# Paired stores at the end of a fused attention and gated feed-forward kernel, with a new order of all its work

## Chip, cores and metric

The kernel runs on one core of one Trainium2 chip. The metric is device time of one execution in microseconds. The engines are TensorE (PE in the profile, with its weight loads as PEld), VectorE (DVE), ScalarE (ACT), GpSimd (POOL) and SyncE (SP). Each runs its own instruction stream in program order and waits on semaphores that other engines raise. SP and POOL also issue the DMA transfers.

## What is computed

Two layers are fused. The first is attention over sequences projected to 64 keys (8 batches, 8 heads, 1024 tokens, 64 wide), the second a gated feed-forward layer on its 8192 tokens (512 to 1536 to 512).

```python
k_proj = einsum('ks,bhsd->bhkd', E, k)
v_proj = einsum('ks,bhsd->bhkd', F, v)
scores = (q @ k_proj^T) / 8
attn   = softmax(scores)                # over the 64 projected keys
x      = attn @ v_proj                  # as [8192, 512] tokens
out    = (sigmoid(x @ w_gate) * (x @ w_val)) @ w_out
```

Inputs and output are float32; the matrices are bfloat16 on the chip.

## The kernel before

The work goes batch by batch. A batch of 1024 tokens is two blocks of 512 tokens, so there are 16 blocks, numbered 0 to 15. For a batch, k and v are loaded and projected (`kv`, `apart`), K and Q are transposed, and four score tiles of 128 token groups go through `score_pair` (PE), `highest` (DVE, the maximum, L1609), `lower` (the subtraction, L1636 on DVE), `exps` (ACT), a DMA transpose on SP (`turn_p`), `outs` (PE), `invert` and `divide` (L1701, L1718; DVE or POOL), and a DMA transpose back (`turn_x`).

The feed-forward products use a seven-product scheme (Strassen's, in Winograd's form): a product of 2x2 sub-blocks takes seven block products instead of eight, with sums of operands before and of results after. For x @ w_gate and x @ w_val, `seven` issues per third of a block and per weight seven products named A11, A12, S2, S1, S3, A22, S4 (jobs GA11, VS4 and so on), each of four matmuls of 256 columns. Between them stand copies of PSUM banks on ACT (`snap`, `copy`, L532), additions on DVE (`plus`, L1104), the tanh on ACT and the gate product on DVE (`hidden`, L1173), which writes hT. For the output layer `o_jobs` issues seven products of twelve matmuls, each split into two jobs of six, with `snap`, `leave` and `copyO` on ACT, `merge` on DVE (L1376), and sums of hidden operands (`s_sum`, L547) on DVE, of which the fourth runs on POOL in three pieces in the inner blocks. The first block runs as plain products (`mm_one`, 512 columns, half products of two matmuls where weights arrive late). All matmuls are issued at L518, all ACT operations at L532.

Eight PSUM banks (pF0 to pF3, pA0 to pA3) and 13 SBUF buffers of 512 columns (EF's two halves and `spare`) hold the intermediate results. They are the scarce resource: a product may start when its bank was read out by the last copy, addition or gate that needs it.

The order is written out by hand of a search. Calls of `job` only collect jobs, each with its engine and body, in the order in which the source makes them. `Scheduler.run` then reads two constant lists. ORDER is a sequence of job numbers; the jobs of each engine are issued in the sequence in which they stand there, and a negative entry -m is a filler, which calls `busy`: one matmul of 256 m columns from the identity into bank 7, whose result nobody reads. PLACES gives every bank or buffer slot its number. `Plan.add` derives from the sequence which operation waits for which, by keys of what each reads and writes; `emit` turns this into semaphore waits (L129; SP's last waits, for the output, at L138).

The output leaves through `ost` (128 x 4 x 512, float32), four token tiles wide. Token tiles are named tt = 0 to 3; tok = tt // 2 is the token half of the scheme, and col = 0 or 1 the half of 512 columns. For blocks 0 to 14, `store` (L1259) sends one token tile of 512 columns, 256 KB, per issue on SP. For the last block `store_half` (L1271) sends one token tile of 256 columns, 128 KB, per issue, eight in all, in the order in which the quarters of the result are ready: (tok 1, col 1) and (tok 0, col 0), then (tok 1, col 0), then (tok 0, col 1), two token tiles each. The last quarter is merged in two pieces, so its two stores wait for one piece each. The kernel ends when SP has waited for the four semaphores out0 to out3.

Of the kernel before, what the change touches and what calls it, by code (L numbers as in the profile page):

```python
# [153 lines left out]
class Job:  # L154
# [191 lines left out]
class Scheduler:  # L346
# [4 lines left out]
    def job(self, eng, pos, body, release=0.0, name=""):  # L351
        self.jobs.append(Job(eng, body, name))
# [24 lines left out]
def bass_linformer_attn__then__ffn_glu_sigmoid_kernel(  # L377
# [20 lines left out]
    with contextlib.ExitStack() as es:  # L398
# [867 lines left out]
        def store_half(blk, tt, col):  # L1266
# [7 lines left out]
                cost=0.4,  # L1274
                nbytes=128 << 10,
            )

        def o_plain(blk, pos, step):
            h = hT[blk % 2]
            last = blk == 2 * B - 1  # L1280
# [616 lines left out]
```

## Time and profile before

| | |
|---|---|
| runs | 516.63, 516.04 and 516.71 us; median 516.63 |
| the profiled execution | 516.16 us, of which its span 514.4 us |
| instructions in the trace | 12647 |
| DMA packets | 140987, 71.60 MB |
| HBM | 60.29 MB read, 16.78 MB written |
| granted TensorE clock | 1.00 |

The span runs from the first to the last instruction of the program. Busy time of an engine is the time in which at least one of its instructions runs. For TensorE matmuls overlap: a matmul of 256 columns has a row of about 0.27 us, though the next one starts much sooner, so the rate is read from the starts of successive rows and not from their lengths. A timeline row gives start, length, engine, line, operation, output tile <- input tiles, shape and count; in brackets stands the idle time before it and what ended that. A row of a stretch gives, after its bounds and length, the busy time of PE, PEld, DVE, ACT and POOL, each with its number of instructions, then the granted clock, the share of DMA engines and GB/s. Names such as pA, pF, spare, ost are tiles without their numbers.

### The profile page before, as it was taken

To read this page: it belongs to the slowest core of one execution; us is meant where nothing else is said; L and a number is where in the kernel's file an instruction comes from. 1 tells how busy PE (TensorE), PEld (TensorE's weight loads), DVE (VectorE), ACT (ScalarE), POOL (GpSimd) and SP (SyncE) were. 2 spreads that over 40 slices of the span, in tenths; PEclk is the share of its full clock that TensorE was granted. 3 is DMA by queue.
4 is the path that set the end of the run, shared out by engine and by line. 5 is a ranking of instruction groups with operands and counts; after the bars stand their busy time and mean duration, and the time that the engine had idled before them with its cause. 6 is when DMAs were issued, how large, how long until landed. Compare 5 with 4: busy or idle time off the path is not lost.

```text
span 514.4 us, 12647 instructions
## 1 busy us (share of the span) xinstructions
PE 508.6 (99%) x4973; PEld 419.1 (81%) x4976; DVE 441.1 (86%) x858; ACT 372.7 (72%) x714; POOL 174.2 (34%) x200
## 2 busy tenths in 40 slices
PE   8999999999999999999999999999999999999997
PEld 4556858888888888888888888888888888888886
DVE  6779998699978997798996998979988899957885
ACT  1567776878887787866877777776888669668662
POOL 9894003623335016230244305350234301350020
PEclk9999999999999999999999999999999999999999
DMA  9999978899887448985699945998577932432004
GB/s 169 197 198 207 182 116 185 128 181 175 148 170 137 74 133 127 215 136 129 106 168 191 160 129 112 169 161 132 137 136 167 191 103 45 103 102 83 2 3 164
DMA packets 140987, 71.60 MB, mean 139 GB/s; under 512 B 97280, under 2 KB 133120, under 8 KB 140928
## 3 DMA queue, kind: packets, MB, share of 16 engines
q0 software_dynamic: 35936, 29.89, 38.9%
q1 hardware_dynamic: 104992, 40.91, 37.5%
q8 instruction: 39, 0.64, 0.5%
q14 instruction: 20, 0.16, 0.1%
HBM read 60.29 MB, written 16.78 MB: 150 GB/s over the span
## 4 chain that ended last, share of the span: by engine, by line
PE 98%; DVE 0%; ACT 0%; issue 0%; DVEq 0%
PE pA L518 51%; PE pF L518 48%; DVE hT L1173 0%; ACT EFT L532 0%; ACT spare L532 0%; ACT qT L532 0%; DVE ost L1376 0%; DVE warm L646 0%; DVE spare L1104 0%; DVE tV L647 0%; DVEq L129 0%
## 5 line engine op out<-in xcount | busy, mean ns | idle before, releaser
L532 ACT ACTIVATE spare<-pA 128x512 f32<-128x512 f32 (+2 forms) x169 | 95.7, 581 | 34.5 <-PE pA L518 22.5
L532 ACT ACTIVATE spare<-pF 128x512 f32<-128x512 f32 (+2 forms) x150 | 83.6, 570 | 33.9 <-PE pF L518 23.8
L547 POOL TENSOR_TENSOR hT<-hT,hS 128x512 bf16<-128x512 bf16 x42 | 48.7, 1174 | 123.2 <-PE pA L518 54.3
L1718 POOL TENSOR_TENSOR KVs<-spare,inv 128x384 bf16<-128x384 f32 (+1 forms) x51 | 37.9, 751 | 77.5 <-ACT spare L532 16.2
L1104 DVE TENSOR_TENSOR spare<-pA,spare 128x512 f32<-128x512 f32 x61 | 41.1, 682 | 15.2 <-PE pA L518 9.7
L532 ACT ACTIVATE spare<-spare 128x512 f32<-128x512 f32 x75 | 45.8, 627 | 2.4 <-DVE spare L1104 2.3
L1173 DVE SCALAR_TENSOR_TENSOR hT<-spare,pA 128x512 bf16<-128x512 f32 x57 | 38.6, 680 | 10.0 <-PE pA L518 8.7
L518 PE MATMUL pF<-wO,hT 128*128 128x256 bf16 (+1 forms) x310 | 43.8, 284 | 0.1
L518 PE MATMUL pA<-xT,wG 128*128 128x256 bf16 (+1 forms) x256 | 41.7, 286 | 0.0
L1173 DVE SCALAR_TENSOR_TENSOR hT<-spare,pF 128x512 bf16<-128x512 f32 x56 | 37.6, 679 | 3.5 <-PE pF L518 2.0
L518 PE MATMUL pA<-wO,hT 128*128 128x256 bf16 (+1 forms) x275 | 37.1, 277 | 0.1
L1104 DVE TENSOR_TENSOR spare<-pF,spare 128x512 f32<-128x512 f32 x50 | 33.9, 682 | 2.7 <-PE pA L518 1.3
L518 PEld LDWEIGHTS pF<-wO,hT 128*128 128x128 bf16 x312 | 30.1, 98 | 7.2 <-ACT pF L532 0.2
L518 PE MATMUL pF<-xT,wV 128*128 128x256 bf16 (+1 forms) x208 | 33.9, 285 | 0.0
L518 PE MATMUL pA<-xT,wV 128*128 128x256 bf16 (+1 forms) x200 | 32.4, 285 | 0.0
L518 PE MATMUL pA<-xS,wV 128*128 128x256 bf16 x208 | 31.0, 273 | 0.1
L518 PE MATMUL pA<-xS,tG 128*128 128x256 bf16 x208 | 31.1, 272 | 0.0
L559 POOL DMA_DIRECT2D Qb<-in_q_dram x18 | 14.2, 787 | 49.5 <-ACT ost L532 22.9
L518 PEld LDWEIGHTS pA<-wO,hT 128*128 128x128 bf16 x276 | 26.5, 98 | 4.3 <-issue 0.2
L518 PEld LDWEIGHTS pA<-xT,wG 128*128 128x128 bf16 x256 | 24.6, 98 | 6.1 <-ACT pA L532 0.3
L518 PE MATMUL pA<-xS,wG 128*128 128x256 bf16 x192 | 28.7, 273 | 0.0
L518 PE MATMUL pF<-wT,hT 128*128 128x256 bf16 x216 | 28.7, 273 | 0.0
(186 smaller groups left out, 1310.9 us busy)
## 6 DMA issues: line engine op xcount, KB each, us to landing
out_dram<-ost SPq DMA_DIRECT2D x60, 256.0 KB, 2.5
KVs<-in_v_dram POOLq DMA_DIRECT2D x15, 512.0 KB, 7.4
KVs<-in_k_dram POOLq DMA_DIRECT2D x14, 512.0 KB, 7.9
Qb<-in_q_dram POOLq DMA_DIRECT2D x14, 512.0 KB, 7.7
wO<-in_moe_w_out_dram POOLq DMA_DIRECT2D x1, 1536.0 KB, 18.7
KVs<-in_k_dram POOLq DMA_DIRECT2D x4, 256.0 KB, 6.4
Qb<-in_q_dram POOLq DMA_DIRECT2D x4, 256.0 KB, 8.5
wG<-in_moe_w_gate_dram POOLq DMA_DIRECT2D x4, 256.0 KB, 10.1
```

Of the source, the lines that this page charges most:

```text
L518: lambda e: e.matmul(o, lhsT, rhs, **kw),
L532: lambda e: e.activation(o, i, func, scale=scale),
L547: fn = lambda e: e.tensor_tensor(o, a, b, op)
L559: add("POOL", lambda e: e.dma_start(o, i), r=r, w=w, dma=sem, cost=0.78, nbytes=nbytes)
L1104: lambda e: e.tensor_tensor(PB(b)[:, :] if stay else BF(s), PB(b)[:, :], BF(s), ALU.add),
L1173: lambda e: e.scalar_tensor_tensor(o, y.rearrange("p (j c) -> p j c", j=2), 1.0, x.rearrange("p (j c) -> p j c", j=2), ALU.add, ALU.mult,),
L1718: fn = lambda e: e.tensor_tensor(xto.rearrange("p (g h d) -> p h g d", g=2, h=H)[:, hh[0] : hh[1], :, :], o[:, :, 0:DH].rearrange("p (h g) ...
```

## The change

For the last block the two token tiles of a quarter are sent by one issue (`store_pair`, 256 KB, 256 runs of 1 KB) for the first three quarters; the last quarter keeps its two single stores. So eight stores become five, and the job count goes from 2917 to 2914. The two constant lists are new: ORDER has 2942 entries instead of 2943, PLACES has 907 as before. No other line of the program changes.

In ORDER, most jobs stand near their old place: on TensorE 733 of 1039 jobs have another position among the jobs of their engine, by 1.9 places on average and 12 at most. The fillers are 22 entries -2 and six -1, where they were 20 and six.

```diff
 ORDER = (
-    16, -2, -2, -2, 17, 18, 4, 19, -2, -2, -2, -1, 28, 20, 29, 1, 30, 21, 31, -2, -1, 22, 0, 32, 2, 38, 33, -2,
...
+    2244, 2074, 2064, 2169, 2075, 2213, 2088, 2068, 2257, 2071, 2246, 2229, 2081, 2207, 2082, 2089, 2083, 2258,
...
 PLACES = (
-    0, 2, 4, 1, 1, 3, 5, 0, 6, 1, 0, 0, 2, 0, 1, 3, 3, 2, 4, 5, 4, 4, 0, 2, 5, 2, 4, 5, 5, 9, 7, 10, 3, 5, 4, 0,
...
+    0, 2, 6, 2, 1, 3, 5, 1, 4, 0, 2, 0, 0, 1, 3, 3, 6, 2, 1, 2, 1, 1, 2, 4, 2, 4, 0, 5, 5, 7, 4, 8, 7, 0, 0, 1,
...
+        def store_pair(blk, tok, col):
+            t = 4 * (blk % 2) + tok
+            cc = slice(256 * col, 256 * col + 256)
+            add(
+                "SP",
+                lambda e: e.dma_start(
+                    out_v[blk // 2, t : t + 3 : 2].rearrange("t p c -> p t c")[:, :, cc],
+                    ost[:, 2 * tok : 2 * tok + 2, cc],
+                ),
+                r=[("ost", 2 * tok + j, col) for j in range(2)],
+                dma=f"out{2 * tok}",
+                cost=0.4,
+                nbytes=256 << 10,
+            )
...
-            for i, tok, col in ((4, 1, 1), (4, 0, 0), (5, 1, 0), (6, 0, 1)) if last else ():
-                for tt in (2 * tok, 2 * tok + 1):
-                    job("SP", pos + step * i, lambda tt=tt, col=col: store_half(blk, tt, col), name="store")
+            for i, tok, col in ((4, 1, 1), (4, 0, 0), (5, 1, 0)) if last else ():
+                job("SP", pos + step * i, lambda tok=tok, col=col: store_pair(blk, tok, col), name="store")
+            for tt in range(2 * last):
+                job("SP", pos + step * 6, lambda tt=tt: store_half(blk, tt, 1), name="store")
```

Entries that the prediction speaks of, as they stand in the two lists for TensorE (numbers are jobs; 84 and 82 transpose Q of the first batch, 86 is a score tile, 143, 149 and 148 are half products of the first block, 2810 is the last product VS4, 2888 reads the gate that follows it):

```
old: 84, 82, 143, 86              new: 84, 82, 149, 148, 86
old: 2810, 2892, 2893, 2895, 2896, 2897, 2898, 2888     (2873 stands between 2810 and 2892)
new: 2810, 2895, 2897, 2898, 2888
```

357 rows, old and new, of tables (ORDER, PLACES) are left out of this document.

## The prediction

> **What bounds the kernel now.** I read the page first, then TensorE's waits, its timeline, and the queues at the end.
>
> ```profile
> span 514.4 us, 12647 instructions
> PE 508.6 (99%) x4973; PEld 419.1 (81%) x4976; DVE 441.1 (86%) x858; ACT 372.7 (72%) x714; POOL 174.2 (34%) x200
> PE 98%; DVE 0%; ACT 0%; issue 0%; DVEq 0%
> ```
>
> The chain that ended last is TensorE from end to end. The matmuls set the time, and an order can only change three things: filler matmuls, moments in which TensorE waits, and what follows its last matmul. The waits of TensorE by what ended them:
>
> ```profile
> PE pA L518 <- DVE tV L647: 1.1, 1, 1.1
> PE pF L518 <- DVE hT L1173: 0.4, 1, 0.4
> PE pA L518 <- ACT qT L532: 0.4, 1, 0.4
> PE pF L518 <- ACT EFT L532: 0.3, 1, 0.3
> ```
>
> That is 2.2 us, and the first 1.1 us is the start before any operand exists. Shorter waits hide in the pipeline: a matmul's row is longer than its issue slot, so I compare starts. The slot first, from the end, where six runs follow without a wait (one is quoted, with its successor):
>
> ```profile
> 508.48 1.47 PE L518 MATMUL pA<-wT,hT 128*128 128x256 bf16 x12
> 509.79 1.47 PE L518 MATMUL pF<-wO,hT 128*128 128x256 bf16 x12
> ```
>
> Twelve matmuls of 256 columns take 1.31 us from start to start, 0.109 us each; four take 0.44 us. Now places where four take longer:
>
> ```profile
> 97.06 0.60 PE L518 MATMUL pA<-xS,tV 128*128 128x256 bf16 x4
> 98.08 0.61 PE L518 MATMUL pF<-xS,wG 128*128 128x256 bf16 x4 [0.42 <-DVE hT L1173]
> ...
> 204.98 0.60 PE L518 MATMUL pA<-xS,wV 128*128 128x256 bf16 x4
> 205.49 0.60 PE L518 MATMUL pA<-xS,tG 128*128 128x256 bf16 x4
> ...
> 272.82 0.60 PE L518 MATMUL pA<-xS,tV 128*128 128x256 bf16 x4
> 273.46 0.61 PE L518 MATMUL pA<-xS,wG 128*128 128x256 bf16 x4
> ...
> 302.63 0.60 PE L518 MATMUL pA<-xT,wV 128*128 128x256 bf16 x4
> 303.12 0.83 PE L518 MATMUL pF<-wO,hT 128*128 128x256 bf16 x6
> ...
> 448.70 0.60 PE L518 MATMUL pA<-xT,wG 128*128 128x256 bf16 x4
> 449.27 0.60 PE L518 MATMUL pA<-xS,tG 128*128 128x256 bf16 x4
> ```
>
> Less 0.44, the waits are 0.58, 0.07, 0.20, 0.05 and 0.13 us. Going through the timeline after 50 us in this way, from the first of these places to the last, I find some twenty, about 2.5 us together. That sum is an estimate from starts that I do not all quote. So from 50 to 511 us an order can gain 2.5 us at most, and lose any amount.
>
> **The change part by part.** I read the two ORDER lists as instruction streams per engine: a non-negative number is a job, the jobs are those of the listing, and PLACES gives each job its bank and buffer. No job but the last stores is added or removed, and shape changes on TensorE (score pairs, projections) come in as many runs as before from the second batch on.
>
> *Filler.* The old list has 20 entries -2 and six -1, the new one 22 and six.
>
> ```profile
> L518 PE MATMUL pA<-ident 128*128 128x512 bf16 x20 | 6.0, 381 | 0.0
> ...
> 26.34 1.03 PE L518 MATMUL pA<-xT,wG 128*128 128x512 bf16 x4
> 27.20 1.03 PE L518 MATMUL pF<-xT,wV 128*128 128x512 bf16 x4
> ```
>
> A slot of 512 columns is (27.20 - 26.34) / 4 = 0.215 us, so two more cost 0.43 us. Below that it can only cost less, down to nothing where operands come late anyway. TensorE shows no wait on a load between 8 and 28 us, so I take **+0.43**.
>
> *First scores.* Scores 86 need the copies of transposes 82 and 84.
>
> ```profile
> 29.37 0.59 PE L518 MATMUL pF<-xT,wV 128*128 128x512 bf16 x2
> 30.36 0.38 PE L518 MATMUL pA<-kpD,qT 128*128 128x128 bf16 x4 [0.39 <-ACT qT L532]
> ```
>
> Between transpose and scores there lies one half product (143), two slots of 0.215 us, and TensorE starts 0.99 us after them instead of 0.43: 0.56 us lost, of which the row calls 0.39 waiting. In the new list two half products (149, 148) lie there. Two more slots cover 0.43: **-0.4** (between 0, if ACT comes later by as much, and -0.56).
>
> *Eight-matmul gaps.* Many waits in the fence are of one kind: a product ends, ACT copies its bank (snap, copyO, leaveO), and a matmul that needs the copy or the bank comes eight matmuls later.
>
> ```profile
> L532 ACT ACTIVATE spare<-pA 128x512 f32<-128x512 f32 (+2 forms) x169 | 95.7, 581 | 34.5 <-PE pA L518 22.5
> ```
>
> Eight slots are 0.87 us; the copy is 0.58, and the last matmul's row ends 0.16 after its slot (four have 0.60 for slots of 0.44). With two handoffs nothing is left, so each such place loses the 0.05 to 0.13 seen at 204.98, 302.63 and 448.70. After 45 us I count 20 places with only eight slots in the old lists (also counting what stands ahead of the copy on ACT), ten in the new, and one with less (scores 2401, about seven slots). Nine fewer at about 0.08: **-0.7**, between -1.2 and 0.
>
> *Waits that come of a queue.* Those at 97.06 and 272.82 are of DVE: the add or the gate was behind other work.
>
> ```profile
> 102.90:205.80 102.90, 102.90 (x1066) 88.20 (x1064) 93.92 (x181) 80.70 (x158) 33.25 (x38) 1.00 0.79 143
> L1104 DVE TENSOR_TENSOR spare<-pA,spare 128x512 f32<-128x512 f32 x61 | 41.1, 682 | 15.2 <-PE pA L518 9.7
> L1173 DVE SCALAR_TENSOR_TENSOR hT<-spare,pA 128x512 bf16<-128x512 f32 x57 | 38.6, 680 | 10.0 <-PE pA L518 8.7 <-PE pF L518 0.6 <-ACT spare L532 0.2
> L1609 DVE TENSOR_REDUCE topf<-pA 128x8 f32<-128x512 f32 x34 | 22.8, 681 | 0.7 <-PE pA L518 0.5
> ```
>
> DVE is busy 93.92 of 102.90 us there (third busy column), and each add (L1104), gate (L1173) or score maximum (L1609) takes 0.68 us, so one that waits for a later product holds up all behind it. Some 1.6 us of the 2.5 are of this kind. For the old waits I compared the slots between the product that the queue waits for and the matmul that needs it: at product 1629 they go from 16 to 20, at 1443 from 16 to 21, at 2485 from 8 to 24; at 1556 (272.82) they stay 22, and at 457 (97.06) they fall from 20 to 16 behind another gate. I take half of 1.6 as gone, -0.8, and +0.5 for waits in places that are now nearer: **-0.3**, with bounds of -1.6 and +3. The upper one is four late DVE operations of 0.68 that nothing covers.
>
> *Loads and transposes.* POOL issues all weight loads ahead of the sums of weights, and wO before batch 1's K.
>
> ```profile
> L559 POOL DMA_DIRECT2D wV<-in_moe_w_val_dram x8 | 6.4, 809 | 0.0
> ...
> DMA  9999999999999999999999999999999999999997
> ```
>
> The last line is the DMA share from 20 to 60 us: the engines are full, so what lands last does not move, and the weights that the new list uses earlier by more than a product (wV's third chunk, wG's fifth) also stand earlier in the queue. Zero, hidden by the plain products; a load that came late would cost at most one place in the queue, 0.8 us of issue. On SP one transpose of batch 2's Q now stands ahead of a store and of the last transpose of batch 1's probabilities. TensorE's list of waits has none on a DMA. Zero; uncovered, it is one issue.
>
> *The end.*
>
> ```profile
> 510.72 0.42 DVE L1376 SCALAR_TENSOR_TENSOR ost<-pF,EF 128x256 f32<-128x256 f32 x1 [1.01 <-PE pF L518]
> 511.37 0.42 DVE L1376 SCALAR_TENSOR_TENSOR ost<-pF,EF 128x256 f32<-128x256 f32 x1 [0.23 <-PE pF L518]
> ...
> 510.70 0.33 SPq L1271 DMA_DIRECT2D out_dram<-ost  x1
> 511.07 0.43 SPq L1271 DMA_DIRECT2D out_dram<-ost  x1
> 511.55 0.46 SPq L1271 DMA_DIRECT2D out_dram<-ost  x1
> 512.05 0.45 SPq L1271 DMA_DIRECT2D out_dram<-ost  x1
> ...
> out_dram<-ost SPq DMA_DIRECT2D x60, 256.0 KB, 2.5
> out_dram<-ost SPq DMA_DIRECT2D x8, 128.0 KB, 1.8
> ```
>
> The last merge ends at 511.79, but its store is issued at 512.05: SP was busy with the three ahead. With a pair in place of the two at 510.70 and 511.07, SP is free by about 511.15, the next half goes at its merge's end (511.14) and is through at 511.6, and the last goes at about 511.84: -0.2. An issue that finds SP idle took 0.33 instead of 0.45, which may give 0.1 more. Against it, the pair's 256 KB land in 2.5 us, from 510.70 at 513.2, beside the last halves; these moved as many bytes before, so I allow +0.2 for it. **-0.25**, between -0.4 and +0.2. The Trainium skill (DMA: Bandwidth & Descriptors, Anatomy of one DMA) has about 2 us of fixed time in every DMA, most of it the receipt of the write. By it merging removes nothing behind the last issue, and its formula gives 2.3 us for 128 KB, an estimate; the row of 128 KB stores has 1.8, so the trace agrees on the kind and is shorter. By this rule alone the term would be the -0.2 of the issue slots.
>
> The order just before the end changes too: the last product VS4 (job 2810) had 42 slots between it and output product 2888, which reads its gate; now it has 18, or 1.96 us. Add 0.68, gate 0.68, drain 0.16 and handoffs make 1.7. It fits by 0.3; one operation of DVE too many costs up to 0.4. Zero.
>
> Sum: +0.43 - 0.4 - 0.7 - 0.3 - 0.25 = **-1.2 us**, on a profiled execution of 516.16 us (span 514.4 and 1.8 around it). The runs shown have a median of 516.63; on that, 515.4.
>
> **The rivals.** *As many waits as before.* New near places take back what the eight-slot gaps and the queue give (-1.0 becomes 0): -0.2, 516.4. For it: such waits depend on all queues together, and I counted places, not queues. Against it: the eight-slot places really are half as many.
>
> *DVE's order makes new waits.* A gate or an add stands on DVE behind an operation whose product comes later; TensorE then loses one operation, 0.68 us, as at 98.08. The place is 103 to 309 us, where score maxima share DVE with the adds and gates. Two such waits undo the gain of 1.2; from four on the kernel is over 0.2% slower. Five give -1.2 + 3.4: 518.8; the likeliest of this case, four, 518.1. For it: DVE is at 91% there. Against: at the places I compared, the distances mostly grew.
>
> *POOL's sums meet DVE's.* The sum that frees the last output product runs on POOL in inner blocks.
>
> ```profile
> L547 POOL TENSOR_TENSOR hT<-hT,hS x42: 1142/1154/1597, 93.5 to 494.2; 128x512 bf16<-128x512 bf16 x42
> ```
>
> Most take 1.15 us, the slowest 1.60. If the new order puts a DVE sum beside each block's POOL sums, a chain of three can be 1.3 us late, as 3 times 0.44; two blocks whose matmuls do not cover it give 516.63 - 1.2 + 2.6 = 518.0, and below one block the forecast stands. The Trainium skill (SBUF — State Buffer, Who interferes with whom) says that a DVE operation with two SBUF inputs and a GpSimd operation that reads SBUF block each other for a whole instruction; the slowest row agrees.
>
> **How the numbers follow.** Forecast 0.40, faster, its own range 514.0 to 515.6. As many waits 0.28, within 0.2%. DVE's order 0.26, slower. POOL's sums 0.06, slower. A measurement of this kernel tells about 0.2%, 1.0 us, from no change. Of the forecast's case 0.02 ends within 0.2%, and 0.02 of the second faster. So faster 0.40, same 0.28, slower 0.32. The range begins where every term lies half way to its lower bound (0.2 - 0.5 - 0.95 - 0.95 - 0.3 = -2.5, so 514.1), rounded to 514.0; all lower bounds together (512.9) would need five lucky terms, and 0.06 is left out there. It ends at 518.4, between four and five uncovered DVE operations, and leaves out 0.12 above.
>
> **What would show it.** Fills: 22 rows of 128x512 from the identity. First scores: no wait on ACT qT over 0.1 at 30 us. Gaps: fewer starts late by 0.05 to 0.13. Queues: TensorE's list of waits without DVE hT of 0.4; several such rows would make the prediction wrong. End: last issue about 0.05 after the last merge, and span less last matmul at 2.9 us instead of 3.1.

## The result, and the profile after

| | before | after |
|---|---|---|
| median of all runs | 516.8 us (22 runs) | 514.86 us (22 runs) |
| middle half of the runs | 516.10 to 517.11 | 514.63 to 515.04 |
| the profiled execution | 516.16 us | 514.63 us |
| its span | 514.4 us | 512.8 us |

The ratio is 0.9965, with a 95% interval of 0.9955 to 0.9975: 1.8 us less (1.3 to 2.3). Forecast was 1.2 us less. The medians of the table differ by 1.9 us. Between the two profiled executions it is 1.53 us. The other 0.4 us of the medians' 1.9 is in the table's second row: the middle half of the runs of before is 1.0 us wide, and their median lies 0.6 above the execution that was profiled; that of after is 0.4 wide, and their median lies 0.2 above.

From the page of the changed kernel, the span, the busy times and the first line of the chain that ended last; then TensorE's waits (who waited, for whom: us in total, times, longest). After line 517 stands for 518 of before, 531 for 532; the lines behind the new function moved by 14 or 15.

```profile
span 512.8 us, 12657 instructions
PE 508.0 (99%) x4978; PEld 421.8 (82%) x4978; DVE 441.5 (86%) x858; ACT 371.2 (72%) x714; POOL 172.0 (34%) x200
PE 98%; DVE 2%; ACT 0%; issue 0%; DVEq 0%
```
```profile
PE pA L517 <- DVE tV L646: 1.1, 1, 1.1
PE pA L517 <- ACT spare L531: 0.6, 1, 0.6
PE pF L517 <- ACT EFT L531: 0.3, 1, 0.3
```

TensorE still ends last, but 2% of the chain is now VectorE: one wait there has grown large enough to lead the chain off TensorE. The waits for hT (0.4) and qT (0.4) of before are gone, and one of 0.6 for a copy in `spare` is new. The first scores, in the timeline:

```profile
29.57 0.59 PE L517 MATMUL pA<-xT,wV 128*128 128x512 bf16 x2
30.00 0.59 PE L517 MATMUL pF<-xT,wG 128*128 128x512 bf16 x2
30.43 0.39 PE L517 MATMUL pA<-kpD,qT 128*128 128x128 bf16 x4
```

Two half-products take 0.43 us each from start to start, and the scores follow with nothing lost, where before lost 0.56. The new wait, in the timelines of TensorE, VectorE, ScalarE and GpSimd:

```profile
370.49 0.60 PE L517 MATMUL pF<-xT,tV 128*128 128x256 bf16 x4
371.71 0.35 PE L517 MATMUL pA<-vpD,eT 128*128 128x130 bf16 x3 [0.62 <-ACT spare L531]
...
367.40 1.22 DVE L546 TENSOR_TENSOR hT<-hT 128x512 bf16<-128x512 bf16 x1
368.55 0.68 DVE L1624 TENSOR_REDUCE topf<-pF 128x8 f32<-128x512 f32 x1
...
371.06 0.17 DVE L1716 RECIPROCAL inv<-pA 128x4 f32<-128x4 f32 x1
...
371.27 0.88 ACT L531 ACTIVATE spare<-pA 128x260 f32<-128x260 f32 x2 [0.68 <-DVE inv L1716]
...
367.19 1.15 POOL L546 TENSOR_TENSOR hT<-hT,hS 128x512 bf16<-128x512 bf16 x1 [12.45 <-PE pF L517]
```

From 370.49 to 371.71 are 1.22 us for four slots of 0.109: 0.79 lost. Read backwards: TensorE's matmul needs a bank that ScalarE copies at 371.27, the copy needs the reciprocal of 371.06, and that is the last of VectorE's row of operations without a pause behind the sum at 367.40. This sum took 1.22 us, where 0.42 is usual, and ended 0.28 after GpSimd's. The end, TensorE's last matmuls, VectorE's last merges, and SP's issues, of which those of line 1282 are pairs; then the row of the single halves from the list of DMA issues (median us to landing last):

```profile
508.59 1.47 PE L517 MATMUL pA<-wO,hT 128*128 128x256 bf16 x12
...
509.52 0.42 DVE L1390 SCALAR_TENSOR_TENSOR ost<-pA,spare 128x256 f32<-128x256 f32 x1 [1.00 <-PE pA L517]
510.17 0.42 DVE L1390 SCALAR_TENSOR_TENSOR ost<-pA,spare 128x256 f32<-128x256 f32 x1 [0.23 <-PE pA L517]
...
509.50 0.37 SPq L1282 DMA_DIRECT2D out_dram<-ost  x1
509.97 0.41 SPq L1270 DMA_DIRECT2D out_dram<-ost  x1
510.62 0.34 SPq L1270 DMA_DIRECT2D out_dram<-ost  x1
```
```profile
out_dram<-ost SPq DMA_DIRECT2D x2, 128.0 KB, 1.9
```

The last merge ends at 510.59, and its store is issued at 510.62: SP was free. The last matmul's row ends at 508.59 + 1.47 = 510.06, where it was 511.26: 1.20 us earlier. The spans are printed to 0.1 us, so what follows the last matmul is taken from the times of the executions: of their 1.53 us, 1.20 lie ahead of that point and 0.33 behind it.

### The profile page after: what moved, and what is told of

The parts are those of the page before. It is cut to its first block, busy times and chain, and to the rows that moved or that the text cites. A ratio compares the mean times of both kernels' runs of the same rounds, so it can differ in the third digit from the quotient of the medians.

```text
span 512.8 us, 12657 instructions
## 1 busy us (share of the span) xinstructions
PE 508.0 (99%) x4978; PEld 421.8 (82%) x4978; DVE 441.5 (86%) x858; ACT 371.2 (72%) x714; POOL 172.0 (34%) x200
## 4 chain that ended last, share of the span: by engine, by line
PE 98%; DVE 2%; ACT 0%; issue 0%; DVEq 0%
PE pF L517 51%; PE pA L517 47%; DVE topf L1624 1%; DVE pF L1651 0%; DVE pA L1651 0%; DVE hT L546 0%; ACT EFT L531 0%; DVE ost L1390 0%; ACT spare L531 0%; DVE warm L645 0%; DVE inv L1716 0%; DVE tV L646 0%; DVEq L129 0%
## 5 line engine op out<-in xcount | busy, mean ns | idle before, releaser
L531 ACT ACTIVATE spare<-pA 128x512 f32<-128x512 f32 (+2 forms) x157 | 87.5, 573 | 30.2 <-PE pA L517 21.5
L517 PE MATMUL pF<-xT,wV 128*128 128x256 bf16 (+1 forms) x240 | 40.2, 289 | 0.0
L1172 DVE SCALAR_TENSOR_TENSOR hT<-spare,pA 128x512 bf16<-128x512 f32 x50 | 33.7, 680 | 5.0 <-PE pF L517 4.1
L517 PE MATMUL pF<-xT,wG 128*128 128x256 bf16 (+1 forms) x216 | 35.1, 286 | 0.0
L517 PE MATMUL pA<-wO,hT 128*128 128x256 bf16 x264 | 34.6, 273 | 0.0
L517 PE MATMUL pF<-xS,tV 128*128 128x256 bf16 x208 | 31.3, 273 | 0.0
L517 PE MATMUL pA<-xT,wG 128*128 128x256 bf16 (+1 forms) x192 | 30.8, 284 | 0.0
L517 PE MATMUL pF<-xS,tG 128*128 128x256 bf16 x200 | 29.8, 273 | 0.0
L517 PE MATMUL pF<-xS,wV 128*128 128x256 bf16 x200 | 29.3, 272 | 0.0
L517 PE MATMUL pA<-wT,hT 128*128 128x256 bf16 x216 | 28.3, 273 | 0.0
## 6 DMA issues: line engine op xcount, KB each, us to landing
KVs<-in_v_dram POOLq DMA_DIRECT2D x15, 512.0 KB, 7.4
KVs<-in_k_dram POOLq DMA_DIRECT2D x14, 512.0 KB, 8.2
Qb<-in_q_dram POOLq DMA_DIRECT2D x14, 512.0 KB, 8.2
```

The source lines that it names most:

```text
L517: lambda e: e.matmul(o, lhsT, rhs, **kw),
L531: lambda e: e.activation(o, i, func, scale=scale),
L1172: lambda e: e.scalar_tensor_tensor(o, y.rearrange("p (j c) -> p j c", j=2), 1.0, x.rearrange("p (j c) -> p j c", j=2), ALU.add, ALU.mult,),
```

## The experiments

The theory: the order gains, not the stores; of the order, first scores, eight-matmul gaps and queue waits each give a part, and one new wait, that of a VectorE sum on a GpSimd sum, takes 0.8 us back. Rivals: the stores carry it; the start, with its fillers, carries it; or the new wait comes of too much work on VectorE, whatever GpSimd does. All runs are compared with the kernel before on the same chip. In the diffs of ORDER a line is the neighbourhood of the entry.

### Stores and order apart

The old ORDER with the paired stores, and the new ORDER with eight single ones:

```diff
 old ORDER, end (stores are 2909 to 2916, with pairs 2909 to 2913)
-2902, 2910, 2891, 2890, 2909, 2903, 2912, 2905, 2911, 2904, 2906, 2907, 2914, 2913, 2908, 2915, 2916
+2902, 2909, 2891, 2890, 2903, 2910, 2905, 2904, 2906, 2907, 2911, 2908, 2912, 2913
 new ORDER, end
-2902, 2891, 2890, 2909, 2903, 2910, 2905, 2904, 2906, 2907, 2911, 2912, 2908, 2913
+2902, 2891, 2890, 2910, 2909, 2903, 2912, 2911, 2905, 2904, 2906, 2907, 2914, 2913, 2915, 2908, 2916
```

> Old order with the paired stores alone. Theory (terms add up): only the end moves, by the 0.25 us of the prediction to the 0.37 us that the profile after shows between last matmul and end; ratio to before 0.9993 to 0.9995. Rival (the end came earlier because the new order's last outputs are ready in another rhythm): no difference, ratio 1.0000, and the last store is still issued 0.2 us or more after the last merge.

> New order with the eight single stores of before. Theory: the order carries the gain without the end, 1.2 us in the profiled executions, so a ratio of about 0.9972, 0.3 to 0.4 us more than the changed kernel. Rival (the pair carries more than its issue slots, because eight issues keep SP from its waits): 0.9985 or above.

| | eight single stores | pairs and two single |
|---|---|---|
| old order | 1 | 0.9994 (0.998 to 1.0008) |
| new order | 0.9969 (0.9958 to 0.9981) | 0.9965 (0.9955 to 0.9975) |

The order, by which both lists are meant (no run parts ORDER from the buffer numbers in PLACES), carries 1.6 us (1.0 to 2.2). What the pairs do can't be told from nothing by time, but it can by the trace: the last merge in the timeline of the old order with pairs; then the last merge in that of the new order with single stores, with SP's last two issues in one row.

```profile
512.22 0.42 DVE L1388 SCALAR_TENSOR_TENSOR ost<-pF,EF 128x256 f32<-128x256 f32 x1 [0.23 <-PE pF L515]
```
```profile
510.51 0.42 DVE L1373 SCALAR_TENSOR_TENSOR ost<-pA,spare 128x256 f32<-128x256 f32 x1 [0.23 <-PE pA L515]
...
510.87 0.96 SPq L1268 DMA_DIRECT2D out_dram<-ost  x2
```

With pairs in the old order, whose span was 514.9, 514.9 - 512.64 = 2.26 us follow the last merge, and 2.2 in the changed kernel. With single stores it is 2.6 before, and here, with a span of 513.7, 513.7 - 510.93 = 2.77: SP begins the last but one store at 510.87, so the last waits for it. As far as spans printed to 0.1 us tell it, the pairs give some 0.3 us in the old order and 0.5 in the new. The first number is smaller than the spread of the old order's runs, and in the profiled execution with pairs in the old order it is hidden: its span is 0.5 longer than that of before, because a load of V, issued at 105.16, landed 9.2 us later, where it took 7.2 before, and TensorE lost 0.8 us at 114. Its row in TensorE's waits:

```profile
PE pF L515 <- DMA KVs<-in_v_dram: 0.4, 1, 0.4
```

### The new wait: two ways to take it away

VectorE's sum one place later, behind the maximum; or GpSimd's sum later, with VectorE's queue as it was.

```diff
-2249, 2238, 2209, 2245, 2052, 2057, 2056
+2249, 2209, 2245, 2052, 2057, 2238, 2056        (2238: VectorE's sum, 2057: the maximum)
```
```diff
-2249, 2238, 2209, 2245, 2052, ... 2070, 2244, 2074
+2249, 2238, 2209, 2052, ... 2070, 2244, 2245, 2074   (2245: GpSimd's sum)
```

> The changed kernel with one VectorE sum of hidden tiles (the 128x512 one that took 1.22 us at 367.40) one instruction later in VectorE's queue, behind the maximum. Theory (that sum started while GpSimd's sum ran, and stood still until GpSimd had ended): the maximum no longer waits for it, TensorE's late start of 0.79 us at 371 goes, 0.7 to 0.8 us less than the changed kernel: span 512.1, ratio about 0.995 to before. Rival (VectorE has too much work there whatever its order): the late start stays, ratio 0.9965.

> The changed kernel with GpSimd's sum that ran from 367.19 to 368.34 moved behind its next one (about 372); VectorE's queue as it was. Theory (VectorE's sum waits for GpSimd's): VectorE's sum at 367.4 takes 0.42 us instead of 1.22, the late start at 371 goes, 0.7 to 0.8 us less than the changed kernel: span 512.1, ratio about 0.995. Rival (VectorE has too much queued there): the late start of 0.8 us stays, ratio 0.9965, and the sum moves its late start to the three GpSimd sums in a row at 372.

VectorE's sum moved: 514.26 us, ratio 0.9956 (0.9944 to 0.9968), span 512.0. GpSimd's sum moved: 514.3 us, 0.9959 (0.9945 to 0.9972), span 512.4; this execution had lost 0.3 us more than the changed kernel by 150 us, in small pieces far from the place. Both intervals hold the changed kernel's ratio too, so by time alone neither is told from it; the place itself is clear. VectorE's and TensorE's timelines of the first, then of the second:

```profile
367.33 0.68 DVE L1622 TENSOR_REDUCE topf<-pF 128x8 f32<-128x512 f32 x1
367.92 0.63 DVE L544 TENSOR_TENSOR hT<-hT 128x512 bf16<-128x512 bf16 x1
...
370.42 0.60 PE L515 MATMUL pF<-xT,tV 128*128 128x256 bf16 x4
370.91 0.35 PE L515 MATMUL pA<-vpD,eT 128*128 128x130 bf16 x3
```
```profile
367.72 0.41 DVE L544 TENSOR_TENSOR hT<-hT 128x512 bf16<-128x512 bf16 x1
368.05 0.68 DVE L1622 TENSOR_REDUCE topf<-pF 128x8 f32<-128x512 f32 x1
...
370.81 0.60 PE L515 MATMUL pF<-xT,tV 128*128 128x256 bf16 x4
371.24 0.34 PE L515 MATMUL pA<-vpD,eT 128*128 128x130 bf16 x3
```

Without GpSimd's sum beside it, VectorE's takes 0.41 us in the same queue between the same neighbours, and TensorE goes on after 0.43 us instead of 1.22. The load on VectorE is the same, so the rival falls. In the first kernel the maximum, which reads a PSUM bank, ran its usual 0.68 us beside GpSimd's sum, and the VectorE sum behind it lost only 0.2. That version had the lowest median of all, 2.3 us less than before, though its interval overlaps that of the changed kernel.

### The first scores

One of the two half-products goes behind the scores; and the reverse in the old order, a second one ahead of them, together with the move of the next section.

```diff
 new ORDER
-149, 198, 83, 148, 145, 86, 102
+149, 198, 83, 145, 86, 148, 102
 old ORDER
-137, 132, 149, 138, ... 150, 145, 86, 195
+137, 132, 138, ... 150, 145, 149, 86, 195
```

> The changed kernel with one of the two half-products ahead of the first scores moved behind them, so that one covers ScalarE's copy of the turned queries as before. Theory (the second half-product is what took the first scores' wait away): a wait for ScalarE's qT of about 0.4 us returns at 30 us, 0.4 to 0.5 us more than the changed kernel: span 513.3, ratio about 0.9974. Rival (the copy had come earlier for another reason): no wait, ratio 0.9965.

> As the kernel with the gate moved, and one half-product of the first block moved to stand ahead of the first scores, so that two cover ScalarE's copy of the turned queries. Theory: TensorE's wait of 0.4 us for qT at 30 us goes as well, 0.45 us less, both moves together 1.0 us: span 513.4, ratio 0.998. Rival (the start is paced by loads, so time gained before 60 us is spent waiting for a load): the wait goes, but the span stays at that of the kernel with the gate alone.

With one half-product in the new order: 515.05 us, 0.997 (0.9958 to 0.9981), span 513.3. TensorE there, and then in the old order with two:

```profile
29.60 0.59 PE L515 MATMUL pA<-xT,wV 128*128 128x512 bf16 x2
30.32 0.38 PE L515 MATMUL pA<-kpD,qT 128*128 128x128 bf16 x4
```
```profile
29.05 1.03 PE L515 MATMUL pF<-xT,wV 128*128 128x512 bf16 x4
30.30 0.40 PE L515 MATMUL pA<-kpD,qT 128*128 128x128 bf16 x4 [0.23 <-DVE qT L752]
```

The loss returns, but only 0.72 - 0.43 = 0.29 of the 0.56. In the old order the second half-product takes away only 0.56 - (1.25 - 0.86) = 0.17, since then VectorE's copy of the other transpose is late. So the cover is one half of the term, and that both copies run earlier in the new order is the other. The old order with both moves had 516.01 us, 0.9993 (0.998 to 1.0006), span 514.0, where the gate's move alone (next section) has 516.1 and 514.4. The theory's 1.0 us less for the two moves did not come: the half-product added 0.1 by the medians.

### The gate behind a sum that waits for a DMA

```diff
 old ORDER
-521, 437, 416, ... 415, 470, 523        (437: sum of x, 470: the gate)
+521, 416, ... 415, 470, 437, 523
```

> The kernel before, order and stores as they were, with one VectorE sum of x (at 97.00, which waited 3.1 us for a transposed tile from DMA) one instruction later, behind the gate that stood behind it. Theory (VectorE's queue, not its load, made TensorE wait there): the 0.59 us at 98 goes, and with it the row DVE hT of 0.4 in TensorE's list of waits; 0.6 us less, span 513.8, ratio 0.999. Rival (given back within the next 200 us because products then wait at other places): ratio 1.000, span 514.4.

516.1 us, ratio 0.9994 (0.9985 to 1.0003), span 514.4. VectorE's timeline, with the gate now first:

```profile
96.77 0.69 DVE L1170 SCALAR_TENSOR_TENSOR hT<-spare,pF 128x512 bf16<-128x512 f32 x1 [2.42 <-ACT spare L529]
97.43 0.43 DVE L544 TENSOR_TENSOR xS<-xT 128x512 bf16<-128x512 bf16 x1
```

The gate starts 0.6 us earlier, and no start is late at 98 us. The median is 0.44 us lower, by the ratio not to be told from no change. By 33 us the profiled execution had lost 0.45 us more than that of before; from there to the end it lost 0.46 less, as 0.3 of the 0.59 came back at 102 us. The rows there, of VectorE and of GpSimd:

```profile
99.88 1.95 DVE L544 TENSOR_TENSOR xS<-xT 128x512 bf16<-128x512 bf16 x1
...
100.35 1.19 POOL L544 TENSOR_TENSOR hT<-hT,hS 128x512 bf16<-128x512 bf16 x1
```

VectorE's sum took 1.95 us, where before it took 1.39, and ended 0.29 after GpSimd's; two additions behind it came late, and with them two of TensorE's products by 0.15 each.

What changed in this kernel is the spread: the middle half of 11 runs lies from 515.98 to 516.19, where that of before lies from 516.03 to 516.96 (29 runs). The same wait differs between executions of the old order; here the rows of the kernels with pairs, with two fillers more, and with the gaps closed (both below):

```profile
PE pF L515 <- DVE hT L1170: 0.5, 1, 0.5
```
```profile
PE pF L515 <- DVE hT L1170: 0.6, 1, 0.6
```
```profile
PE pF L515 <- DVE hT L1170: 0.7, 1, 0.7
```

Before had 0.4. VectorE stood for the landing of a transpose. By starts the place cost 0.59 us before and 0.70, 0.81 and 0.88 in these three, so it explains 0.3 us of difference between executions. It is not the only such place: the load of V above cost 0.8 us in one execution alone, and the stores of the next section up to 0.8. And the kernel with both moves holds the gate first as well, and the middle half of its runs is 0.6 wide (515.76 to 516.37). So the spread comes in part from this wait; that the move alone narrowed it is not shown.

### Eight-matmul gaps alone

Of the 20 matmuls with only eight slots of cover in the old order, 12 were moved one or two TensorE jobs later; one of them:

```diff
-1547, 1610, 1614, 1471, ... 1624, 1535, 1468, 1548
+1547, 1610, 1471, ... 1624, 1535, 1468, 1614, 1548
```

> The kernel before, order and stores as they were, but 12 of the 20 matmuls of eight-slot places (the product that writes a bank ends only eight matmuls ahead of the matmul that needs ScalarE's copy of it) stand one or two TensorE jobs later. Theory (the small late starts of about 0.08 us at such places are a part of the gain of the new order): 12 x 0.08 = about 1.0 us less, span about 513.4 instead of 514.4, ratio about 0.998 to before. Rival (these starts are given back, or the gain lies only in the waits that the profile names): ratio 1.000, span 514.4.

518.18 us, 1.004 (1.0026 to 1.0054), span 516.4: 2 us slower, against the theory and its rival. All 12 places are on time, as intended, but they held only 0.51 us together. In its profiled execution other losses stand against them: 0.3 us by 7 us, 0.3 more at the wait of 98 us, 0.42 and 0.37 at 151 to 153, 0.36 at 210, and 0.67 instead of 0.24 at 283. TensorE's row of the last, and ScalarE's at 151:

```profile
PE pA L515 <- DVE hT L1170: 0.5, 1, 0.5
```
```profile
151.31 0.60 ACT L529 ACTIVATE ost<-pF 128x512 f32<-128x512 f32 x1 [0.78 <-DMA out_dram<-ost]
```

At 283 it is a moved product: issued later, it ended later for VectorE, which stood 2.3 us for its addition, and the gate that TensorE needs is queued behind that. Those at 151 to 153 are of another kind. ScalarE's copy into `ost` stood 0.78 us for an output store that landed 4.3 us after its issue, where before none near it took over 2.4; the kernel with two fillers more, which lacks these moves, has the same wait with 0.55 us and a landing after 4.1. So of the 2 us of this one execution the moves account for some of it, and why all five runs are 2 us slower stays open.

### Fillers and the start

From the changed kernel two or all 28 fillers were taken away, or two added, and two were added in the old order. Results of fillers are read by nobody.

```diff
 new ORDER, two fewer
-63, -2, -2, -2, -1, 129, ... 14, -2, 64
+63, -2, -2, -1, 129, ... 14, 64
 new ORDER, two more
-14, -2, 64
+14, -2, -2, -2, 64
 old ORDER, two more
-14, -2, -2, -1
+14, -2, -2, -2, -2, -1
```

> Changed kernel without two of its 512-column fillers, both after the last V load of the first batch. Theory: each costs its slot of 0.215 us, so 0.43 us less than the changed kernel, ratio to before about 0.9957. Rival (the start is paced by loads and copies, fillers only fill): the same 0.9965, and waits of 0.4 us appear behind the removed fillers.

> Changed kernel without all 28 fillers (22 x 0.215 + 6 x 0.109 = 5.4 us of slots). Theory: most fillers stand where operands have not come, so TensorE waits instead, and the gain is some 0.4 us, no more than the spare time behind the first landings; ratio to before 0.9955 to 0.9965. Rival 1 (every filler costs its slot): 5.4 us less, ratio 0.986. Rival 2 (without the fillers the granted clock is lower for a while): slower than the changed kernel by 1 us or more, with a clock below 1.00 in the first 20 us.

> The kernel before with two fillers of 512 columns more at 21 us and nothing else. Theory A (TensorE paces the start, as the prediction had it): 2 x 0.215 = 0.43 us more, span 514.8, ratio 1.0008. Theory B (loads pace it, as the kernels with fewer fillers suggest): the two slots come off later waits, span 514.4, ratio 1.000.

> The changed kernel with two fillers of 512 columns more at 22 us and nothing else: the same disturbance that gave the old order 0.5 us by 33 us and 0.8 us of new waits behind that. Theory (what the new order gains is mostly that it keeps its time when a transfer or the start shifts): TensorE's list of waits stays as it is, at most the two slots are paid, 0.43 us: span 512.8 to 513.2, ratio 0.9965 to 0.9973, and half of all runs within 0.5 us. Rival (the new order is as sensitive as the old one and was only lucky in its profiled execution): new waits of 0.3 to 0.9 us after 60 us, span 513.6 to 514.1, ratio 0.998 to 0.999, half of all runs spread over 1 us.

| | median | ratio to before | span |
|---|---|---|---|
| new, two fewer | 514.69 (5 runs) | 0.996 (0.9946 to 0.9973) | 512.9 |
| new, none | 515.3 (12 runs) | 0.9969 (0.9957 to 0.9981) | 514.4 |
| new, two more | 515.18 (7 runs) | 0.9969 (0.9958 to 0.998) | 513.4 |
| old, two more | 517.03 (12 runs) | 1.0 (0.9991 to 1.0009) | 515.6 |

Two fewer put TensorE 0.47 us ahead at 33 us, of which 0.33 were there by 7 us, before any filler that was taken away; the start differs by as much between executions of other kernels too. It then stands at the first scores of batch 1, at 67 us:

```profile
66.33 0.60 PE L515 MATMUL pF<-xT,tG 128*128 128x256 bf16 x4
67.20 0.20 PE L515 MATMUL pA<-kpD,qT 64*128 64x64 bf16 x1 [0.27 <-DMA qT<-Qb]
```

0.87 us for four slots, where the changed kernel takes 0.53: 0.34 are back, in a wait for a transposed Q, and the last 0.13 go at 142 us. Without any filler, 22 x 0.215 + 6 x 0.109 = 5.4 us of slots are gone, and by 25 us TensorE has lost about 5.0 us more in waits. The granted clock is 1.00 there too, in the first 25 us as well, so the rival that it would fall without fillers did not come, nor did the one by which all 5.4 us are gained. Its 12 runs fall into two groups of six, 514.26 to 514.77 and 515.84 to 516.40; the first is 0.3 us below the changed kernel. The profiled one is of the second, with this row in TensorE's waits, and this in VectorE's timeline; then what the view of `ost` says of its two stores from 280 to 300 us (us to landing), in this kernel and in the changed one:

```profile
PE pF L514 <- DVE ost L1387: 1.2, 1, 1.2
```
```profile
297.40 0.69 DVE L1387 SCALAR_TENSOR_TENSOR ost<-pF,spare 128x512 f32<-128x512 f32 x1 [1.57 <-ACT vpD L528]
```
```profile
DMA to landing us min/median/max: 3.9/5.1/6.3
```
```profile
DMA to landing us min/median/max: 2.8/3.3/3.8
```

The merge waits for its part of `ost` to be sent. ScalarE, which the row names, had ended at 297.07; the store issued at 290.99 landed 6.3 us later, at 297.3, beside a load of 512 KB on POOL's queue. TensorE lost 1.39 us at that place; the groups lie 1.6 apart. No execution of the faster group was profiled, so that this store parts the groups is not shown. The same execution lost 0.24 us at 274, where VectorE's sum stood 0.48 us for a transposed tile: the new order has a sum that waits for a DMA as well.

Two fillers more set both orders back at first. The old one then also meets new waits, at 98 us (0.81 instead of 0.59), at 151 to 153 (0.56 together) and at 174 (0.17): from 33 us on it loses 0.8 us more than before. Those at 151 to 153 are of the late store told above, so the fillers need not be their cause. The new one loses the same 0.1 us from 33 us on as the changed kernel, and its span is longer by 0.6, the two slots and 0.1 of the start. (Its page counts 4977 matmuls and 4980 weight loads; the three missing rows look like late starts of one slot, as at the end of this text, and are not counted as such.) The ratios alone don't tell the two cases apart. The middle half of the new order's 7 runs is 0.2 us wide, that of the old one's 12 runs 1.0, and that of the new order's 12 runs without fillers 1.5.

## Why the prediction was right

The forecast's case came: faster, 514.86 where 515.4 was predicted in a range from 514.0 to 518.4. The terms, against the two profiled executions:

- **Filler, +0.43: mis-sized.** The two slots are paid by 33 us. Of what two fewer gained, nothing is left at the end; two more cost 0.6 us of span and 0.2 by ratio; and without all 28 the faster half of the runs is 0.3 us better and all runs together 0.2 worse by ratio. The text had the bound ("down to nothing where operands come late anyway") and dismissed it because TensorE's list shows no wait on a load between 8 and 28 us. The fillers are why it shows none: they stand where such waits would be. And the place where the gain went back was at 67 us, outside the stretch looked at. So removing fillers gives next to nothing, while two added ones were paid in full.
- **First scores, -0.4:** 0.56 in the rows. The second half-product explains 0.29 of it; the rest is that both copies come earlier.
- **Eight-matmul gaps, -0.7:** late starts at the 20 places counted add up to 1.04 us before, and at those of the new order, scores 2401 with 0.13 among them, to 0.45: -0.6. As a recipe it failed: closing 12 of them by hand went with 2 us more. The new order has fewer of them without such a loss; which of its other moves see to that is not shown.
- **Queue waits, -0.3:** gone are 0.59 at 98 us and 0.20, 0.24 and 0.15 at 273, 282 and 251, together 1.18; new is 0.79 at 371: -0.4. The sizes assumed, half of 1.6 gone and +0.5 new, were each too small by about 0.3 us, so that the net is near the forecast is luck. The 0.20 at 273 is absent from the five other profiled executions of the old order, so it is not the order that took it away, and the order's part is 0.98 gone. The distances misled at 457, where slots fell and the wait went as well.
- **Loads and transposes, zero:** no wait for a DMA is in the list of after.
- **The end, -0.25:** -0.33 between the two executions, about -0.3 with the pairs alone. The last issue came 0.03 us after the merge (0.05 forecast), where before it came 0.26 after; that is 0.23. The last issue itself took 0.34 instead of 0.45 us, the 0.1 that had been allowed for. The 0.2 allowed against it, for the pair's bytes beside the last halves, did not come. The formula that the prediction takes from the Trainium skill (DMA: Bandwidth & Descriptors, Anatomy of one DMA) stands there for a DMA issued by GpSimd. These stores are issued by SP, and the sum did not use it.
- **VS4, zero:** no late start among the last products.

Added up: 0.43 - 0.56 - 0.6 - 0.4 - 0.33 = -1.5, with 0.2 more lost before 7 us, where both kernels wait for first operands and executions of one order differ by as much, and 0.2 less in pieces too small to name. The difference of the profiled executions is 1.53 us, against 1.2 predicted.

The rest of the gain is in no term. The prediction worked from one execution of before and took the others to lie a constant above it. But the other executions of the old order lose more at DMA transfers that land late: at the gate behind a sum that waits for one (0.59 to 0.88 us, which the new order avoids), at a load of V (0.8), at stores (up to 0.8). How much each adds to the spread of before's runs is not shown, as each kernel has one profile. That the new order keeps its time better is supported by the spreads of few runs, and without fillers it did not.

Of the rivals, *GpSimd's sums meet VectorE's* cost TensorE 0.79 us at one place, without the chain of three sums that its price assumed. Such meetings are not new: nine VectorE operations are prolonged beside a GpSimd sum in the trace of before, eight in that of after, of which the one at 367.40 alone cost TensorE a wait. The rival was given 0.06 as a loss that decides the sign. It did not decide, but it is the largest single wait the new order brought; by the traces taking it away is worth 0.8 us, by time no more than the intervals allow. *VectorE's order* is what the hand-closed gaps show at 283 us, with 0.43 of their 2 us; *as many waits* did not come.

## What to carry to other kernels

Cover that one place lacks is taken from another: a matmul moved later is also a product that comes later for the engine that waits for it, so count both ends before moving one. An operation that waits for a DMA should stand behind, not ahead of, work that is ready, since its wait differs between executions and one profile may show too little of it; that holds also for a write into a staging tile whose last store has not landed, which cost TensorE 0.8 and 1.39 us here. A filler in a stretch paced by loads hides the waits that it stands for; what it costs is known when it is taken out and the trace read further on.

## What the runs showed of the hardware

A VectorE operation with two operands in SBUF that starts while a GpSimd sum runs seems not to slow down but to stand until GpSimd has ended, and then to run. At 367.40 it ended 0.28 us after GpSimd's end (368.34) and took 1.22 instead of 0.42. The other prolonged ones of before and after end as late, 0.28 to 0.29 us after GpSimd's end with 512 columns of bfloat16 and 0.55 to 0.56 with 1024 or in the gates, which take float32, wherever in GpSimd's sum they began, from 0.09 to 0.89 us after its start; a mere slowing would not give one and the same distance. Before has the same at 91.64 us, in VectorE's and GpSimd's timelines; and after has the reverse order, where VectorE's sum started first:

```profile
91.64 1.34 DVE L547 TENSOR_TENSOR xS<-xT 128x512 bf16<-128x512 bf16 x1
...
91.55 1.15 POOL L547 TENSOR_TENSOR xS<-xT,xS 128x512 bf16<-128x512 bf16 x1
```
```profile
277.96 0.69 DVE L546 TENSOR_TENSOR hT<-hT 128x1024 bf16<-128x1024 bf16 x1
...
278.13 1.54 POOL L546 TENSOR_TENSOR hT<-hT,hS 128x512 bf16<-128x512 bf16 x1 [3.67 <-PE pA L517]
```

There VectorE keeps its 0.69, and GpSimd takes 1.54 instead of 1.15. The Trainium skill (SBUF — State Buffer, Who interferes with whom) says that a VectorE instruction with two SBUF inputs contends with a GpSimd instruction that reads SBUF, and that the port pair they share is an exclusive lock; at these places the trace agrees in both directions. One place does not fit: at 99.88 us of the kernel with the gate first, VectorE's row starts 0.5 us ahead of GpSimd's and still ends 0.29 after it, and the kernel with both moves has the same at 99.37; why is open. VectorE lost up to 1.0 us at one operation of these two traces, and at 367 us an operation that reads PSUM, set ahead of the sum, brought that down to 0.2.

One caution for reading starts. In the timeline of before stand

```profile
63.73 0.61 PE L518 MATMUL pF<-ident,kpd 128*128 128x128 bf16 x8
64.39 0.81 PE L518 MATMUL pA<-wO,hT 128*128 128x512 bf16 x3
```

Eight slots of 128 columns end at 64.17, and the next row seems 0.22 late. But the group has four matmuls, and 0.215 is one slot of 512: the first one's record is missing, and nothing was lost.
